# Two feed-forward units woven into the last attention steps, and a new order of the work that follows

## The chip, the cores and the metric

The kernel runs on one core of one Trainium2 chip. The metric is the device time of one execution in microseconds (us); a smaller number is better. A kernel's time is the median of its runs.

## What is computed

Four batches of eight heads go through attention with rotary positions, and the result goes through a SwiGLU layer (a matrix product with a gate weight and one with a value weight, the SiLU of the first times the second, and a product with an output weight). All inputs and outputs are 32-bit floats.

```python
scores = np.matmul(q_rot, k_rot.transpose(0, 1, 3, 2)) / np.sqrt(D)      # 4 x 8 x 576 x 576, D = 64
attn = np.exp(scores - np.max(scores, axis=-1, keepdims=True))
attn = attn / (np.sum(attn, axis=-1, keepdims=True) + 1e-09)
x = np.matmul(attn, v)                      # then transposed and reshaped to 2304 tokens x 512
g = x @ w_gate                              # 512 x 1536
val = x @ w_val                             # 512 x 1536
out = (g * (1 / (1 + np.exp(-g))) * val) @ w_out                         # 1536 x 512
```

## The kernel before, in words

Each 32-bit operand of a product is split into a high and a low part (names that end in `h` and `l`), and a product is the sum of three: high by high, high by low, low by high. ScalarE (ACT) writes the high part by a cast, and VectorE (DVE) or GpSimd (POOL) writes the low part by a subtraction.

**Attention** works on 16 pairs of heads with nine blocks each. A block has scores on TensorE (PE), the negated maximum on DVE (L375), the exponential on ACT (L393), transposes on PE (L436) with their split on ACT and DVE (L437, L438), and the products with the values on PE (`pv_some`, L476, ten matmuls to a group). `pv_evac` copies a finished group to `Y` and stores it to the DRAM tensor `yd`. The row sums become reciprocals `rt`, and `rstore` transposes them, copies them and stores them to the DRAM tensor `rd`.

**The plain stage** (`plain`) computes twelve units: two blocks `f` of 128 of the 1536 columns, by six blocks of 384 tokens, which `UNITS` lists as (f, s, t). A unit is two chains of twelve matmuls (`mm`, L772), one with the gate weight `w0`, one with the value weight `w1`. Then `ev` takes both out of PSUM on ACT: a SiLU (L779), a copy (L780) and one or two stores (L787, L790). PSUM holds three units, so a unit's matmuls wait for the `ev` of the unit three places before it. In the text, ev(u) is the evacuation of unit u. In the listing below, unit 0 is `ps` of `attn_swiglu`.

What stands between the units prepares the next stage:
- `wfirst(1, i)` splits the weights of f = 1. Its DVE part is L733 to L739, its ACT part L720, its POOL part L721 and L722. The raw weights lie in the buffer `raw0`, which `ev` of some units uses afterwards as `sv`.
- `forms` (POOL, L700) makes sums of token blocks in the tiles `T0l0` and `T0l1`, for which `T1` then casts and subtracts (L694). `T0l0` takes over room in which attention's `ET2l` lay.
- `yload` and `rload` fetch attention's results and reciprocals (SyncE's queue, SP). `xlate(t)` scales and splits the token block t = 1 or 2 of the second half (`x1`, `x2` in `plain`; L665 to L680) in small alternating steps of ACT and DVE.
- `Stream` prepares raw weights one block at a time, through two buffers: `load` starts a DMA (L758), `sign` is an ACT operation at the head of a block (L734), and `take` adds the six DVE operations (L735 to L740). `take` signs the next block in the midst of this one unless its second argument is false, and ends with a `load` into the buffer that has come free.
- `sums` (POOL) and `split` (ACT, POOL) make the weights of the first Strassen unit; `forms2` makes `T2`.

**The Strassen stage** (`strassen`, L812) forms the other ten blocks' products from seven products per step. One product is a chain of six matmuls, each chain has one of six PSUM buffers, and DVE's additions (L796) and ACT's copies (L815) free them. **The last stage** (`finish`) multiplies by the output weights.

The order of the work from the end of attention on is written out by hand in `attn_swiglu`, `plain` and `strassen`: each engine takes its instructions in the order in which these functions name them, and an instruction that waits holds up all behind it on its engine. The DMA queues are in order too.

Of the kernel before, what the change touches and what calls it, by code (L numbers as in the profile page):

```python
# [10 lines left out]
FP32 = mybir.dt.float32  # L11
# [112 lines left out]
class Attn:  # L124
# [362 lines left out]
    def store(self, p, half, Y):  # L487
        d = (self.nc.scalar if (p, half) == (B * H // 2 - 1, 1) else self.nc.sync).dma_start
        b, c = divmod(p, 4)
        s, bb = divmod(b, 2)  # L490
        m = s * SG + bb * 512 + 256 * half
        t = s * SG + 1024 + bb * 64
        yd = self.yd[:, 2 * c:2 * c + 2].rearrange("h a d q -> (a d) h q")
        if half == 0:
            d(out=yd[:, :, m:m + 256], in_=Y)
            return
        self.done.add(p)
        Y = Y.rearrange("p h q -> p (h q)")
# [20 lines left out]
class Moe:  # L519
# [113 lines left out]
    def xload(self, s, c, t):  # L633
        o = s * SG + t * BK
        X = self.ld_p.tile([128, 2, BK], FP32, name="Xab")
        for h in range(2):
            self.nc.sync.dma_start(out=X[64 * h:64 * h + 64],
                                   in_=self.yd[h, 2 * c:2 * c + 2, :, o:o + BK].rearrange("a d q -> d a q"))
        return X[:, 0], X[:, 1]

    def xprep(self, s, c, t, ld, eng):
# [4 lines left out]
        self.hicopy(eng, hi, Xa)  # L646
        eng.tensor_tensor(out=lo, in0=Xa, in1=r32(hi), op=ALU.subtract)

    def yload(self, t, c0, c1):
        o = SG + t * BK  # L650
        for h in range(2):
            src = self.yd[h, :, :, o:o + BK].rearrange("(c a) d q -> a d c q", a=2)
            for a, Y in enumerate((self.Ya, self.Yb)):
                self.nc.sync.dma_start(out=Y[64 * h:64 * h + 64, t - 1, c0:c1], in_=src[a, :, c0:c1])

    def xlate(self, t):
        nc = self.nc
# [115 lines left out]
                n += 1  # L773
        return ps

    def ev(self, f, s, t, ps, sv):
        nc = self.nc
        sv = sv.rearrange("p (t i q) -> p t i q", i=2, q=128)
# [183 lines left out]
def attn_swiglu(ctx: ExitStack, tc: tile.TileContext, qk, vr, wg, wv, wo, tab, out):  # L962
    nc = tc.nc
    dr = ctx.enter_context(tc.tile_pool(name="dr", bufs=1, space=bass.MemoryType.DRAM))
    yd = dr.tile([2, 2 * NCH, D, NT], FP32, name="yd")
    rd = dr.tile([B, 36, 128], FP32, name="rd")
    hd = (dr.tile([NFF, 128, FT, 2, 128], FP32, name="hf"), dr.tile([18 - FT, 128, NFF, 2, 128], FP32, name="ht"))
    NP = B * H // 2
# [120 lines left out]
    scx.close()  # L1089
    cctx, xctx = ExitStack(), ExitStack()  # L1090
    moe.open_chain(cctx, 4)
    at.trans(NB - 1)
    at.pv_some(10)
    at.pv_evac()
    at.tails(NP - 1, 1)
    ps = [moe.mm(0, 0, 0, 0)]
    at.pv_some(10)
    at.pv_evac()
    for op in cv1[1]:
        op()  # L1100
# [12 lines left out]
    pl.close()
    moe.open_mid(mctx)
# [11 lines left out]
def run(ops, n=99):  # L1126
    while ops and n:
        ops.pop(0)()
        n -= 1
# [34 lines left out]
        return out  # L1164


def plain(moe, ps):
# [16 lines left out]
    for f in (0, 1, 2, 3, 7, 8, 9, 10, 11):  # L1184
        job("o", f)
    S = Stream(moe, jobs)
    ps, sv = {0: ps}, {}

    def mm(u):
        f, a, t = UNITS[u]  # L1190
        ps[u] = [moe.mm(f, a, t, i) for i in range(2)]

    def ev(u):
        if u % 4 == 0:
            raw = moe.again("raw0", [128, 2, 2 * BK], FP32, "sv")
            sv[u], sv[u + 1] = raw[:, 0], raw[:, 1]
        elif u % 4 > 1:
            sv[u] = moe.ld_p.tile([128, 2, BK], FP32, name="Xab").rearrange("p a q -> p (a q)")
        moe.ev(*UNITS[u], ps.pop(u), sv.pop(u))
# [46 lines left out]
    run(x2)
    ev(7)
    mm(9)
    run(moe.forms2(ve))
# [115 lines left out]
```

## Time and profile before

| quantity | value |
|---|---|
| time, median of 3 runs | 732.16 us (732.03 to 732.17) |
| the profiled execution's own time | 734.16 us |
| its span | 732.4 us |
| PE busy | 703.4 us, 96% of the span |
| DVE busy | 550.8 us, 75% |
| POOL busy | 465.5 us, 64% |
| ACT busy | 405.9 us, 55% |
| PE's share of the chain that ended last | 73% |

The span is the time from the first to the last recorded instruction, and the execution's own time lies 1.8 us above it. The profiled execution took 2.0 us longer than the median run. Busy shares are averages over stages. The granted clock is TensorE's: 1.00 stands for 2.4 GHz and 0.50 for 1.2 GHz, and a value between says how long it was at either.

### The profile page before, as it was taken

To read this page: it belongs to the slowest core of one execution; us is meant where nothing else is said; L and a number is where in the kernel's file an instruction comes from. 1 tells how busy PE (TensorE), PEld (TensorE's weight loads), DVE (VectorE), ACT (ScalarE), POOL (GpSimd) and SP (SyncE) were. 2 spreads that over 40 slices of the span, in tenths; PEclk is the share of its full clock that TensorE was granted. 3 is DMA by queue.
4 is the path that set the end of the run, shared out by engine and by line. 5 is a ranking of instruction groups with operands and counts; after the bars stand their busy time and mean duration, and the time that the engine had idled before them with its cause. 6 is when DMAs were issued, how large, how long until landed. Compare 5 with 4: busy or idle time off the path is not lost.

```text
span 732.4 us, 12724 instructions
## 1 busy us (share of the span) xinstructions
PE 703.4 (96%) x4356; PEld 662.1 (90%) x4356; DVE 550.8 (75%) x898; ACT 405.9 (55%) x884; POOL 465.5 (64%) x462
## 2 busy tenths in 40 slices
PE   6699999999999998988999999999999999999997
PEld 6589999999999998888999999999999977888887
DVE  5799888888888889647987877878766895465451
ACT  2588988888888887336652433324334333333331
POOL 4696989999899957766867675557674857300000
PEclk9999999999999999999999999999999999999999
DMA  4888788779887885783446464665647965787671
GB/s 146 235 204 219 185 191 248 201 200 251 215 207 207 224 208 192 194 225 125 137 145 178 153 188 145 191 183 152 180 123 215 310 250 187 287 278 237 210 216 30
DMA packets 111585, 144.12 MB, mean 197 GB/s; under 512 B 17808, under 2 KB 86432, under 8 KB 111520
## 3 DMA queue, kind: packets, MB, share of 16 engines
q1 hardware_dynamic: 106816, 137.51, 65.5%
q10 hardware_dynamic: 4704, 5.79, 2.4%
q8 instruction: 35, 0.57, 0.3%
q14 instruction: 30, 0.25, 0.1%
HBM read 76.61 MB, written 42.54 MB: 163 GB/s over the span
## 4 chain that ended last, share of the span: by engine, by line
PE 73%; DVE 10%; DMA 6%; ACT 5%; SPq 2%; issue 1%; POOL 1%; ACTq 0%; DVEq 0%; POOLq 0%
PE ch L812 30%; PE ch L929 13%; PE pv L476 9%; PE sc L360 8%; PE tr L436 6%; PE ch L880 3%; DMA HF<-hf 2%; ACT E L393 2%; DVE nmt L375 1%; PE tr L299 1%; DMA X<-in_qk_dram 1%; ACT N L318 1%; DMA hf<-sv 1%; DMA QZ<-N 1%; DVE HF L870 1%
## 5 line engine op out<-in xcount | busy, mean ns | idle before, releaser
L375 DVE TENSOR_REDUCE nmt<-sc 128x1 f32<-128x576 f32 x144 | 108.0, 752 | 21.1 <-PE sc L360 19.9
L393 ACT ACTIVATE E<-sc,nmt 128x576 f32<-128x576 f32 x128 | 97.4, 761 | 11.9 <-DVE nmt L375 10.2
L796 POOL TENSOR_TENSOR u<-u,z 128x384 f32<-128x384 f32 x30 | 30.5, 1016 | 76.6 <-DVE sg L796 76.6
L436 PE MATMUL tr<-ident,E 128*128 128x128 f32 x512 | 77.0, 273 | 0.6 <-DVE N L322 0.6
L815 ACT COPY c<-ch 128x384 f32<-128x384 f32 x30 | 14.4, 481 | 93.2 <-issue 47.1
L360 PE MATMUL sc<-QK 128*128 128x288 f32 x248 | 61.6, 330 | 3.0 <-DMA QK<-N 1.4
L436 PEld LDWEIGHTS tr<-ident,E 128*128 128x128 f32 x512 | 61.3, 141 | 2.8 <-PE tr L299 1.3
L224 POOL TENSOR_TENSOR t<-X,tabs 128x256 f32<-128x256 f32 (+1 forms) x90 | 51.8, 597 | 16.6 <-DMA X<-in_qk_dram 7.2
L694 DVE TENSOR_TENSOR hl<-hg,hh 128x384 fp32r<-128x384 f32 x44 | 25.8, 587 | 38.6 <-ACT hh L694 38.6
L360 PE MATMUL sc<-N,QZ 128*128 128x288 f32 x248 | 53.6, 298 | 1.1 <-DMA QZ<-N 1.1
L929 PE MATMUL ch<-Oh,hh 128*128 128x512 f32 (+1 forms) x144 | 54.0, 375 | 0.0
L437 ACT CAST ET2h<-tr 128x512 fp32r<-128x512 f32 x80 | 47.1, 589 | 12.4 <-PE tr L436 12.4
L929 PE MATMUL ch<-Oh,hl 128*128 128x512 f32 (+1 forms) x144 | 53.9, 374 | 0.0
L929 PE MATMUL ch<-Ol,hh 128*128 128x512 f32 (+1 forms) x144 | 53.8, 374 | 0.0
L438 DVE TENSOR_TENSOR ET2l<-tr,ET2h 128x512 fp32r<-128x512 f32 x80 | 53.1, 683 | 0.6 <-ACT ET2h L437 0.6
L228 POOL TENSOR_TENSOR rot<-rot,t 128x512 f32<-128x512 f32 (+1 forms) x45 | 45.8, 1017 | 3.5
L796 DVE TENSOR_TENSOR sg<-ch,u 128x384 f32<-128x384 f32 x60 | 33.4, 557 | 18.9 <-PE ch L812 15.7
L438 DVE TENSOR_TENSOR ET1l<-tr,ET1h 128x512 fp32r<-128x512 f32 x64 | 42.8, 685 | 6.4 <-ACT ET1h L437 6.2
L437 ACT CAST ET1h<-tr 128x512 fp32r<-128x512 f32 x64 | 36.4, 598 | 17.7 <-PE tr L436 14.5
L227 POOL TENSOR_TENSOR rot<-X,tabs 128x512 f32<-128x512 f32 (+1 forms) x45 | 45.5, 1010 | 0.0
L360 PEld LDWEIGHTS sc<-QK 128*128 128x128 f32 x248 | 38.5, 192 | 6.6 <-ACT E L393 4.6
L694 ACT CAST hh<-hg 128x384 fp32r<-128x384 f32 x44 | 22.6, 514 | 38.5 <-DVE hg L916 38.5
(409 smaller groups left out, 2429.5 us busy)
## 6 DMA issues: line engine op xcount, KB each, us to landing
QK<-N SPq DMA_DIRECT2D x62, 288.0 KB, 4.8
hg<-ht SPq DMA_DIRECT2D x22, 768.0 KB, 6.2
HF<-hf SPq DMA_DIRECT2D x12, 896.0 KB, 5.1
X<-in_qk_dram SPq DMA_DIRECT2D x15, 576.0 KB, 6.7
yd<-Y SPq DMA_DIRECT2D x31, 256.0 KB, 3.8
ht<-sg SPq DMA_DIRECT2D x20, 384.0 KB, 2.9
hf<-sg SPq DMA_DIRECT2D x20, 384.0 KB, 3.6
ht<-sg SPq DMA_DIRECT2D x20, 320.0 KB, 2.8
```

Source lines behind the costliest of these rows:

```text
L224: ins = e.tensor_tensor(out=sel(t2, u), in0=sel(x, w), in1=tb(Sn, u), op=ALU.mult)
L360: nc.tensor.matmul(ps[:, g, 0:288], l, rr[:, o + g * 288:o + (g + 1) * 288], start=(x == 0), stop=(x == len(terms) - 1))
L375: nc.vector.tensor_reduce(out=nmcol, in_=ps[:, :, 0:288], axis=AX.XY, op=ALU.max, negate=True)
L393: nc.scalar.activation(out=E.rearrange("p (a b) -> p a b", a=2), in_=ps[:, :, 0:288], func=ACTF.Exp, bias=nmcol, scale=1.0, accum_out=self ...
L436: nc.tensor.transpose(ps[:, c], E[:, o + c * 128:o + (c + 1) * 128], self.ident)
L437: nc.scalar.copy(dst[0], src)
L438: nc.vector.tensor_tensor(out=dst[1], in0=src, in1=r32(dst[0]), op=ALU.subtract)
L476: nc.tensor.matmul(st["ps"][:, 0:w], VS[:, sl, :], t, start=(x == 0), stop=(x == last))
L694: return [lambda: self.nc.scalar.copy(h, f), lambda: le.tensor_tensor(out=l, in0=f, in1=r32(h), op=ALU.subtract)]
L796: add = lambda e, out, in0, in1: e.tensor_tensor(out=out, in0=in0, in1=in1, op=ALU.add)
L812: nc.tensor.matmul(acc, l[:, w, c * 128:(c + 1) * 128], r, start=(n == 0), stop=(n == 5))
L929: self.nc.tensor.matmul(ps, l[:, f], r[:, z], start=(n == 0), stop=(n == 3 * NFF - 1))
```

## The change

It touches the last steps of attention and the plain stage.
- The first unit's gate chain moves ahead of attention's last transposes, and its value chain ahead of the last two groups of `pv`. The second unit, (0, 0, 1), which was the first one in `plain`, is now woven around the last group: its gate chain ahead of it and its value chain behind it. `ev` of unit 0 and `rstore` stand between the two groups of `pv`.
- `yd` becomes two DRAM tensors, of six and of two of its eight rows per half. `rload` for t = 1 moves ahead of the later `yload` calls.
- The rest of the preparation of w1 of f = 1 (`cv1[1]`, now `first`) moves from the end of attention into `plain`, behind the `forms` and the first `sign`.
- `ev` decides itself which buffer it writes: units 2, 3, 8 and 9 share `raw0`, the others take buffers of `ld_p`.
- Of the stream's weight blocks, one stood in the middle of the stage; it now stands at the end, where two follow each other. `x1` and `x2` move ahead of `T1`, of the splits of the Strassen weights and of `forms` for the first half.

```diff
-    yd = dr.tile([2, 2 * NCH, D, NT], FP32, name="yd")
+    yd = [dr.tile([2, n, D, NT], FP32, name=f"yd{n}") for n in (6, 2)]
...
+    ps = [moe.mm(0, 0, 0, 0)]
     at.trans(NB - 1)
     at.pv_some(10)
     at.pv_evac()
     at.tails(NP - 1, 1)
-    ps = [moe.mm(0, 0, 0, 0)]
+    ps.append(moe.mm(0, 0, 0, 1))
+    at.pv_some(10)
+    moe.ev(0, ps)
+    at.pv_evac()
+    at.rstore(B - 1)
+    ps = [moe.mm(0, 0, 1, 0)]
     at.pv_some(10)
     at.pv_evac()
-    for op in cv1[1]:
-        op()
-    ps.append(moe.mm(0, 0, 0, 1))
-    at.pv_some(10)
-    at.pv_evac()
-    at.rstore(B - 1)
+    ps.append(moe.mm(0, 0, 1, 1))
...
+        if u in (2, 8):
+            raw = self.again("raw0", [128, 2, 2 * BK], FP32, "sv")
+            self.sv = [raw[:, 1], raw[:, 0]]
+        if u in (2, 3, 8, 9):
+            sv = self.sv.pop()
+        else:
+            sv = self.ld_p.tile([128, 2, BK], FP32, name="Xab").rearrange("p a q -> p (a q)")
...
     for c in range(2):
         run(moe.forms(1, c, moe.Z[c], po))
     x1, x2 = moe.xlate(1), moe.xlate(2)
-    mm(1)
+    mm(2)
     S.sign()
-    ev(0)
-    mm(2)
+    run(first)
     run(S.take(1))
     ev(1)
     mm(3)
...
     S.load()
     S.load()
-    for t in (1, 2):
-        moe.yload(t, 0, 3)
-    for t in (1, 2):
-        moe.yload(t, 3, 4)
-        moe.rload(1, t, moe.R12 if t == 2 else None)
+    moe.yload(1, 0)
+    moe.rload(1, 1)
+    moe.yload(2, 0)
+    moe.yload(1, 1)
+    moe.rload(1, 2, moe.R12)
+    moe.yload(2, 1)
...
     mm(4)
-    T1(0)
-    run(x1, 3)
     ev(3)
     mm(5)
-    run(x1)
+    run(x1, 5)
     ev(4)
     mm(6)
-    T1(1)
-    S.sign()
-    run(S.take(1, False))
-    w = [J[0].split(x, po) for x in range(2)]
-    run(w[0])
+    run(x1)
     ev(5)
     mm(7)
-    run(w[1])
+    T1(0)
     run(x2, 3)
     ev(6)
     mm(8)
+    w = [J[0].split(x, po) for x in range(2)]
+    run(w[0])
+    run(x2, 2)
+    ev(7)
+    mm(9)
+    run(w[1])
+    run(x2)
+    T1(1)
...
-    S.sign()
     ev(9)
     mm(11)
+    S.sign()
     run(S.take(1))
     ev(10)
+    run(S.take(1))
     run(J[1].sums(po))
     ev(11)
```

**POOL at the end of attention.** `w1h` and `w1l` are the halves of w1 of f = 1, `T0l` the tiles of the two `forms` (the number tells the two tiles apart), `WF` that of `sums`. Before:

```order
L721 TENSOR_TENSOR raw<-raw,w1h_4089 128x512
L722 TENSOR_TENSOR w1l_4090<-raw 128x512
L700 TENSOR_TENSOR T0l_4436<-xa1h,xa1l 128x2x384
L700 TENSOR_TENSOR T0l_4436<-xm1h,xm1l 128x384
L700 TENSOR_TENSOR T0l_4436<-xb1h,xb1l 128x384
L700 TENSOR_TENSOR T0l_4436<-T0l_4436 128x768
L700 TENSOR_TENSOR T0l_4436<-T0l_4436 128x384 x2
```

And of the change:

```order
L701 TENSOR_TENSOR T0l_4458<-T0l_4458 128x384 x2
L701 TENSOR_TENSOR T0l_4459<-xa1h,xa1l 128x2x384
L701 TENSOR_TENSOR T0l_4459<-xm1h,xm1l 128x384
L701 TENSOR_TENSOR T0l_4459<-xb1h,xb1l 128x384
L701 TENSOR_TENSOR T0l_4459<-T0l_4459 128x768
L701 TENSOR_TENSOR T0l_4459<-T0l_4459 128x384 x2
L722 TENSOR_TENSOR raw<-raw,w1h_4090 128x512
L723 TENSOR_TENSOR w1l_4091<-raw 128x512
L958 TENSOR_TENSOR WF_4456<-WF_4456 128x256
```

The two operations that finish w1 of f = 1 stood ahead of both `forms`; they moved behind the last of their twelve operations.

**ACT at the end of the plain stage**, from ev(9) to ev(11). `aux<-raw` is a block's `sign`, `ACTIVATE sv<-ch` or `Xab<-ch` with its `COPY` is an `ev`, and `c<-ch` is the Strassen stage's first copy. Before:

```order
L734 ACTIVATE aux<-raw 128x512
L779 ACTIVATE sv<-ch 128x3x128
L780 COPY sv<-ch 128x3x128
L790 DMA ht<-sv 128x3x256
L734 ACTIVATE aux<-raw 128x512
L779 ACTIVATE Xab<-ch 128x3x128
L780 COPY Xab<-ch 128x3x128
L790 DMA ht<-Xab 128x3x256
L779 ACTIVATE Xab<-ch 128x3x128
L780 COPY Xab<-ch 128x3x128
L790 DMA ht<-Xab 128x3x256
L815 COPY c_4981<-ch 128x384
```

And of the change:

```order
L788 ACTIVATE sv<-ch 128x3x128
L789 COPY sv<-ch 128x3x128
L799 DMA ht<-sv 128x3x256
L735 ACTIVATE aux<-raw 128x512 x2
L788 ACTIVATE Xab<-ch 128x3x128
L789 COPY Xab<-ch 128x3x128
L799 DMA ht<-Xab 128x3x256
L735 ACTIVATE aux<-raw 128x512
L788 ACTIVATE Xab<-ch 128x3x128
L789 COPY Xab<-ch 128x3x128
L799 DMA ht<-Xab 128x3x256
L824 COPY c_4983<-ch 128x384
```

Before, one `sign` stood ahead of ev(9) and one ahead of ev(10). Now none stands ahead of ev(9), two stand ahead of ev(10), and a third stands between ev(10) and ev(11).

**DVE at the start of the Strassen stage.** `T2l` is the last result of `forms2`, `WF` that of a weight block, and `u<-ch` the first addition of the Strassen stage. Before:

```order
L709 TENSOR_TENSOR T0h<-T0h 128x768
L694 TENSOR_TENSOR T2l<-T0h,T2h 128x2x768 x2
L735 TENSOR_SCALAR aux<-aux 128x512
L736 TENSOR_SCALAR aux<-aux 128x512
L737 SCALAR_TENSOR_TENSOR raw<-raw,aux 128x512
L738 TENSOR_SCALAR aux<-raw 128x512
L739 SCALAR_TENSOR_TENSOR aux<-raw,aux 128x512
L740 TENSOR_TENSOR WF_4435<-raw,aux 128x512
L796 TENSOR_TENSOR u<-ch,c_4981 128x384
```

And of the change, from `forms2` to the end of the first weight block; six more operations of the second block follow, and then the same `u<-ch`:

```order
L695 TENSOR_TENSOR T1l<-T0l_4459,T1h 128x4x384
L710 TENSOR_TENSOR T0h<-T0h 128x768
L695 TENSOR_TENSOR T2l<-T0h,T2h 128x2x768 x2
L736 TENSOR_SCALAR aux<-aux 128x512
L737 TENSOR_SCALAR aux<-aux 128x512
L738 SCALAR_TENSOR_TENSOR raw<-raw,aux 128x512
L739 TENSOR_SCALAR aux<-raw 128x512
L740 SCALAR_TENSOR_TENSOR aux<-raw,aux 128x512
L741 TENSOR_TENSOR WF_4457<-raw,aux 128x512
```

Two blocks of six operations now stand between `T2l` and `u` where one stood, and the second half of `T1l` has come ahead of `forms2`.

## Rows read from the trace of the kernel before

**Rows 1.** Windows: us; busy of PE, PEld, DVE, ACT, POOL (x instructions); clock; DMA.

```profile
360.00:380.00 20.00, 20.00 (x117) 20.00 (x116) 18.62 (x31) 10.82 (x15) 16.39 (x12) 1.00 0.45 138
...
291.00:295.00 4.00, 4.00 (x18) 4.00 (x16) 3.41 (x6) 0.97 (x2) 3.23 (x3) 0.57 0.22 66
...
325.00:329.00 4.00, 3.74 (x12) 3.74 (x13) 2.37 (x5) 2.70 (x8) 0.00 (x0) 0.57 1.13 281
...
341.00:345.00 4.00, 3.17 (x12) 3.18 (x13) 3.33 (x7) 2.42 (x6) 3.92 (x4) 0.69 0.58 199
```

**Rows 2.** Timeline of PE: start, us, instruction, idle time before it and its releaser.

```profile
290.58 0.66 PE L436 MATMUL tr<-ident,Et 128*128 128x128 f32 x4 [1.86 <-ACT Et L393]
...
298.61 0.31 PE L476 MATMUL pv<-ET2h,VS 128*128 128x320 f32 x1
...
306.06 0.44 PE L772 MATMUL ch<-xa1h,w0h 128*128 128x384 f32 x1 [1.56 <-ACT sv L779]
...
310.33 0.34 PE L772 MATMUL ch<-xa0h,w0h 128*128 128x384 f32 x1
...
325.26 0.53 PE L772 MATMUL ch<-xm1h,w0h 128*128 128x384 f32 x1 [2.29 <-ACT Xab L779]
...
341.82 0.44 PE L772 MATMUL ch<-xa2h,w0h 128*128 128x384 f32 x1 [2.06 <-ACT Xab L779]
...
357.67 0.35 PE L812 MATMUL ch<-xa1h,W0h 128*128 128x384 f32 x1
```

**Rows 3.** Timeline of POOL, the same columns.

```profile
300.71 1.54 POOL L721 TENSOR_TENSOR raw<-raw,w1h 128x512 f32<-128x512 f32 x1 [3.98 <-ACT w1h L720]
...
303.60 1.82 POOL L700 TENSOR_TENSOR T0l<-xa1h,xa1l 128x768 f32<-128x768 f32 x1
...
311.42 1.86 POOL L700 TENSOR_TENSOR T0l<-xa1h,xa1l 128x768 f32<-128x768 f32 x1
...
339.99 1.81 POOL L700 TENSOR_TENSOR R<-xa0h,xa0l 128x768 f32<-128x768 f32 x1
...
358.22 1.01 POOL L700 TENSOR_TENSOR Z<-Z 128x384 f32<-128x384 f32 x1
```

**Rows 4.** Timeline of DVE, the same columns.

```profile
293.36 0.63 DVE L438 TENSOR_TENSOR ET2l<-tr,ET2h 128x512 fp32r<-128x512 f32 x1
...
314.25 2.60 DVE L694 TENSOR_TENSOR T1l<-T0l,T1h 128x1536 fp32r<-128x1536 f32 x1 [1.37 <-ACT T1h L694]
...
323.35 0.57 DVE L667 TENSOR_TENSOR aux<-aux,R 128x384 f32<-128x384 f32 x1 [6.03 <-DMA R<-rd]
...
330.75 0.56 DVE L675 TENSOR_TENSOR xa2l<-aux,xa2h 128x384 fp32r<-128x384 f32 x1 [0.47 <-ACT T0h L674]
...
333.40 1.76 DVE L694 TENSOR_TENSOR T1l<-T0l,T1h 128x1536 fp32r<-128x1536 f32 x1 [2.09 <-ACT T1h L694]
...
339.32 0.56 DVE L666 TENSOR_TENSOR aux<-aux,T2h 128x384 f32<-128x384 f32 x1
...
349.73 1.72 DVE L709 TENSOR_TENSOR T0h<-T0h 128x768 f32<-128x768 f32 x1
...
357.19 0.69 DVE L735 TENSOR_SCALAR aux<-aux 128x512 f32<-128x512 f32 x1
...
361.43 0.55 DVE L796 TENSOR_TENSOR u<-ch,c 128x384 f32<-128x384 f32 x1
```

**Rows 5.** Timeline of ACT and its queue, the same columns.

```profile
331.89 1.48 ACT L694 CAST T1h<-T0l 128x1536 fp32r<-128x1536 f32 x1 [0.40 <-ACT sv L780]
...
333.84 1.04 ACT L694 CAST W0h<-WF 128x1024 fp32r<-128x1024 f32 x1
...
356.01 0.64 ACT L734 ACTIVATE aux<-raw 128x512 f32<-128x512 f32 x1 [0.44 <-ACT sv L780]
```

**Rows 6.** DMA: line L758's times to landing; the waits of SP's queue, 285 to 372.

```profile
DMA to landing us min/median/max: 3.2/3.7/7.0
...
SPq L654 <- DMA hf<-sv: 6.8, 1, 6.8
```

More of the change, by code (lines that the diff above doesn't have):

```diff
@@ L492, in store @@
         t = s * SG + 1024 + bb * 64
-        yd = self.yd[:, 2 * c:2 * c + 2].rearrange("h a d q -> (a d) h q")
+        yd = self.yd[c // 3][:, 2 * (c % 3):2 * (c % 3) + 2].rearrange("h a d q -> (a d) h q")
         if half == 0:
@@ L637, in xload @@
             self.nc.sync.dma_start(out=X[64 * h:64 * h + 64],
-                                   in_=self.yd[h, 2 * c:2 * c + 2, :, o:o + BK].rearrange("a d q -> d a q"))
+                                   in_=self.yd[c // 3][h, 2 * (c % 3):2 * (c % 3) + 2, :, o:o + BK].rearrange("a d q -> d a q"))
         return X[:, 0], X[:, 1]
@@ L647, in xprep, with yload @@
         eng.tensor_tensor(out=lo, in0=Xa, in1=r32(hi), op=ALU.subtract)
-    def yload(self, t, c0, c1):
+    def yload(self, t, i):
         o = SG + t * BK
+        z = slice(3 * i, 3 + i)
         for h in range(2):
-            src = self.yd[h, :, :, o:o + BK].rearrange("(c a) d q -> a d c q", a=2)
+            src = self.yd[i][h, :, :, o:o + BK].rearrange("(c a) d q -> a d c q", a=2)
             for a, Y in enumerate((self.Ya, self.Yb)):
-                self.nc.sync.dma_start(out=Y[64 * h:64 * h + 64, t - 1, c0:c1], in_=src[a, :, c0:c1])
+                self.nc.sync.dma_start(out=Y[64 * h:64 * h + 64, t - 1, z], in_=src[a])
     def xlate(self, t):
@@ L774, in mm, with ev @@
         return ps
-    def ev(self, f, s, t, ps, sv):
+    def ev(self, u, ps):
         nc = self.nc
+        f, s, t = UNITS[u]
+        if u in (2, 8):
[5 more added lines that the diff above has]
+            sv = self.ld_p.tile([128, 2, BK], FP32, name="Xab").rearrange("p a q -> p (a q)")
         sv = sv.rearrange("p (t i q) -> p t i q", i=2, q=128)
@@ L1110, in attn_swiglu @@
     moe.open_aux(xctx, 2)
-    J, S, Z = plain(moe, ps)
+    J, S, Z = plain(moe, ps, cv1[1])
     mctx.close()
@@ L1164, in take, with plain @@
         return out
-def plain(moe, ps):
+def plain(moe, ps, first):
     nc = moe.nc
@@ L1186, in plain @@
     S = Stream(moe, jobs)
-    ps, sv = {0: ps}, {}
+    ps = {1: ps}
     def mm(u):
-        f, a, t = UNITS[u]
-        ps[u] = [moe.mm(f, a, t, i) for i in range(2)]
+        ps[u] = [moe.mm(*UNITS[u], i) for i in range(2)]
     def ev(u):
[L1194 to L1199, printed above, removed]
+        moe.ev(u, ps.pop(u))
     def T1(c):
@@ L1245, in plain @@
         run(moe.forms(0, c, Z[c], po))
[L1246 to L1249, printed above, removed]
+    T2 = moe.forms2(ve)
+    run(T2, 2)
     ev(8)
     mm(10)
-    S.sign()
+    run(T2)
     ev(9)
     mm(11)
+    S.sign()
     run(S.take(1))
     ev(10)
+    run(S.take(1))
     run(J[1].sums(po))
```

## The prediction

> **What bounds the kernel now.** I read the windows of all engines first, then PE's timeline around the end of attention, then the timelines of the engines that it waits for. In the Strassen stage PE is full: 117 matmuls in 20.0 us, so a chain of six takes 1.03 us, at a granted clock of 1.00 [rows 1]. Whatever moves the start of that stage therefore moves the end of the kernel by as much. The plain stage ahead of it isn't full. A unit of two chains needs 4.16 us (306.06 to 310.33, less 0.11 for its slow first matmul), but PE stands still for 1.86 us ahead of the last transposes, and for 1.56, 2.29 and 2.06 us ahead of units that find no free PSUM buffer because ACT is late with an evacuation [rows 2]. That is 7.8 us. The granted clock tells the rest: after three of these waits it is 0.57 to 0.69 over four microseconds, between its levels of 1.2 and 2.4 GHz, and twelve matmuls take 3.74 us in place of 2.08 [rows 1]. Such a stretch costs 1.66 us. What made ACT late is on DVE: the first scaling of a late token block waits 6.0 us for the reciprocals `R` [rows 4].
>
> So there is something to win, nearly 13 us with the three slow stretches, and the change aims at the right waits. The question is what waits instead. The orders printed above answer it, and each later step is taken from them.
>
> **The sum, step by step.** Times are on the profile's own axis.
>
> 1. *End of attention.* The chain that now stands ahead of the last transposes covers the 1.86 us wait, and with it goes the slow stretch, 1.66 us. One more chain, 2.08 us, comes ahead of the last group of `pv`, and the transposes of the reciprocals, 0.1 us. The first of the two groups now comes so early that it waits for `ET2l`, which DVE ends at 293.99 [rows 4]: 0.6 us. So the last group starts at 298.61 [rows 2] - 1.86 - 1.66 + 2.08 + 0.1 + 0.6 = 297.9 in place of 298.6. The stores of `rd` and the loads of `R` come several microseconds earlier and are nobody's last wait any more. Splitting `yd` by itself I cost at nothing: its bytes and its DMA count are the same, and where a load may start earlier nobody waits for it.
>
> 2. *POOL.* The first `forms` writes into room that `ET2l` held, so it waits for eight matmuls of that last group, 1.2 us: 299.1. One `forms` took 7.82 us (303.60 to 311.42) [rows 3], two take 15.6, to 314.7. Only then come the two operations that finish w1 of f = 1. They took 2.89 us (300.71 to 303.60) [rows 3], so `w1l` is there at 317.6. Before, it was there at 303.6.
>
> 3. *PE waits for it.* From 297.9 PE does the ten `pv` matmuls (1.5), the second unit's value chain (2.1), unit 2 (4.2), a chain and two matmuls of unit 3 (2.4): it stands at 308.1, until 317.6. What step 1 wins therefore counts only through POOL's start. Ten matmuls of the broken chain follow at the lower clock, 3.2 us, and eight units, 33.3 us. The Strassen stage could start at 354.2, against 357.67 [rows 2]: 3.5 us earlier.
>
> 4. *ACT and DVE behind it.* ev(2) writes to `raw0`, where w1's raw weights lie, so ACT waits for `w1l` too, and then, in ev(3), for the chain that ends at 320.9. The first addition of `x1` starts at about 322.5. `x1` took 8.0 us (323.35 to 331.31): 330.5. ev(5) and the cast of `T1h` (331.89 to 333.40 before [rows 4, 5]) come first again, 2.9 us, then `T1l`, 1.76 us: 335.1. `x2` took 10.4 us (339.32 to 349.73) and now has two casts of `W0h` in ACT's stream, some 0.95 us each from start to start of 1.04 us: 347.4. The second `T1l` comes next; beside a working POOL it took 2.60 us, else 1.76 [rows 4]. I take 2.60, since POOL does the other `forms` then: 350.0. `forms2` with both `T2l` took 7.46 us (349.73 to 357.19): 357.5. The six operations of the first weight block took 4.24 (357.19 to 361.43 [rows 4]): 361.7. Before, one such block had been done in the middle of the stage.
>
> 5. *The load behind it.* The third `sign` needs raw weights whose DMA can be issued only when this block has freed its buffer. Such a load takes 3.7 us (3.2 to 7.0) [rows 6]: 365.4. The sign itself takes 0.64 [rows 5], and ev(11) stands behind it on ACT with 0.48: its first buffer is free at 366.5. PE needs that buffer for the fifth chain of the Strassen stage, at 354.2 + 4.1 = 358.3. It stands still for 8.2 us and then runs a slow stretch, 1.66 us more.
>
> Before, the fifth chain began at 357.67 + 4.1 = 361.8. Now its equal is 366.5 + 1.66 = 368.2. The sum is +6.4 us. DVE's second weight block, ahead of `u`, ends at about 366 and frees the eighth chain's buffer by 367; since PE comes there after 370, it adds nothing. The profiled execution took 734.16 us and would take 740.6; the median of the runs lies 2.0 us below it, so I predict 732.16 + 6.4 = 738.6 us.
>
> *Unknown prices.* ACT's stores and SP's loads share eight completion counters, and one DMA waits until the eighth before it has landed: SP once stood 6.8 us for a store of ACT's [rows 6]. With the new order three of ACT's stores stand behind loads of `yd` and `rd`. ACT had no such wait before, so I take 0 and keep 6.8 as the other end. The casts of `W0h` may be hidden (-1.9), DVE may meet less of POOL (0.84 at `T1l`; `T2l` at `T1l`'s 1.76 each, with half of `forms2`, some 3 us), the load may take 3.2 (-0.5) or 7.0 (+3.3).
>
> *Two rules beside the rows.* `forms` on POOL met DVE's weight operations from 304 to 311 and took 7.82 us; the pair from 339.99 to 359.23 [rows 3], beside `forms2` and `T2l`, took 19.2, against 15.6. The Trainium skill, "SBUF — State Buffer", section "SBUF: two separate sides", says that GpSimd and VectorE share a pair of ports as an exclusive lock that is held for the whole instruction. The longer pair agrees with it, the shorter one shows no trace of it. By the lock the `forms` of step 2 would take up to 19.2 us; that is the second rival.
> For step 5, the row's median is 3.7 us. The Trainium skill, "DMA: Bandwidth & Descriptors", section "Anatomy of one DMA — SWDGE (gpsimd) path", fits 2.0 us plus bytes over 436e3 for another issuing path. For 512 KB I estimate 3.2 us from it, the row's minimum, and the sum would be +5.9.
>
> **The rivals.**
> - *The load isn't waited for, so the kernel is faster.* If ACT and DVE run through `x1`, `x2` and `forms2` with hardly a gap, the first weight block ends early enough for the load to land before PE's fifth chain, and only step 3 counts: -3.5 us, 728.7. It decides from there: step 4's chain has to end by 353.5 in place of 361.7. For it: the work alone, without gaps, is about 31 us of the 39 that I count. Against it: `x1` and `x2` took 8.0 and 10.4 us before, with the same ping-pong between the two engines, and nothing in the change shortens it. 8 in 100.
> - *`forms` takes 19.2 us.* POOL's operations of step 2 meet DVE's weight operations. Everything behind is 3.6 us later: +10.0, 742.2. Against it is the first pair of before, beside the same kind of work. 8 in 100.
> - *About the same.* Half of step 4's gaps go and the collisions with them, some 6 us: +0.4, 732.6. 11 in 100.
> - *The change does what its order is for*, since POOL is quick and w1 is never waited for: the four waits and slow stretches go, and about 9 of 13 us come through: 723. The printed order of POOL speaks against it. 3 in 100.
>
> **How the numbers follow.** 0.2% is 1.5 us, about what a measurement of this kernel can tell from no change. The forecast has 70 in 100, and with the second rival the slower cases have 78. Same has 11, faster 8 + 3 = 11. The range leaves out the faster cases and the far end of slow loads: 733.5, where the third rival begins to turn into the forecast with a few of the low ends, to 743.0, which takes in the second rival. About 18 in 100 lie outside.
>
> **What would show it.** POOL's first `forms` starts near 299 and `w1l` ends near 317.6; PE has one wait of nearly 10 us for POOL's `w1l`, near 308; ACT's first `sv` starts with it. PE waits a second time, near 358, for an evacuation into `Xab`, some 8 us, and ACT's longest wait there is for the DMA of raw gate weights. The granted clock falls after both. The wait of DVE for `R` is gone. The prediction is wrong if `w1l` is ready before 312, or if ACT's third sign doesn't wait for its load.

## The result: 1.2% slower, by two waits in a row

| quantity | before | after |
|---|---|---|
| time, median of 4 runs | 732.15 us (732.03 to 732.17) | 741.00 us (740.53 to 741.51) |
| ratio of the times, 95% interval | 1 | 1.0121 (1.0104 to 1.0139) |
| the profiled execution's own time | 734.16 us | 741.51 us |
| its span | 732.4 us | 739.7 us |
| PE busy | 703.4 us, 96% | 699.4 us, 95% |
| DVE busy | 550.8 us | 553.1 us |
| POOL and ACT busy | 465.5 and 405.9 us | 465.6 and 405.8 us |

The change costs 8.85 us. No engine has more work to do: DVE is busy 2.3 us longer, POOL and ACT within 0.1 us of before, and the time is idle time of PE. The last `ET2l` of attention ends at 292.01 in the profile of after and ended at 293.99 in that of before [rows 4]; so 2.0 us are to be taken off a time on before's axis before it is set beside one of after. On that common axis the profiled spans differ by 739.7 - 730.4 = 9.3 us.

### The profile after

The waits, 285 to 375 us: who waited for whom, us in total, times, longest.

```profile
ACT sv L788 <- POOL w1l L723: 13.7, 1, 13.7
...
PE ch L773 <- POOL w1l L723: 10.4, 1, 10.4
ACT aux L735 <- DMA raw<-in_moe_w_gate_dram: 9.2, 1, 9.2
...
PE ch L821 <- ACT Xab L788: 8.2, 1, 8.2
```

PE waits twice, 10.4 and 8.2 us. Before, it had five waits: the four of 1.56 to 2.29 us [rows 2], and one of 1.09 us at 353.40 that the prediction leaves out. Each of the two waits of after goes with a longer one of ACT, for POOL's `w1l` and for the load of raw gate weights. DVE no longer waits for `R`, as it did for 6.0 us [rows 4].

The timeline of PE over the same stretch: only these instructions were waited for by PE or start a stage.

```profile
292.07 0.41 PE L476 MATMUL pv<-ET2l,VS 128*128 128x320 f32 x1 [0.26 <-DVE ET2l L438]
...
316.43 0.69 PE L773 MATMUL ch<-xa0h,w1l 128*128 128x384 f32 x1 [10.45 <-POOL w1l L723]
...
353.29 0.35 PE L821 MATMUL ch<-xa1h,W0h 128*128 128x384 f32 x1
...
365.83 0.69 PE L821 MATMUL ch<-T1h,W0h 128*128 128x384 f32 x1 [8.18 <-ACT Xab L788]
```

The wait of 1.86 us ahead of the last transposes [rows 2] is gone, as the change intends. The Strassen stage starts at 353.29, against 357.67 - 2.0 = 355.67 before: 2.4 us earlier in spite of the wait of 10.45 us. Everything is lost again, and more, at its fifth chain.

The granted clock in both places, by windows (columns as in [rows 1]):

```profile
312.00:316.00 4.00, 0.00 (x0) 0.00 (x0) 0.63 (x1) 0.00 (x0) 3.84 (x4) 0.50 1.10 232
316.00:320.00 4.00, 3.57 (x11) 3.57 (x12) 0.00 (x0) 0.86 (x2) 3.17 (x5) 0.50 1.04 205
...
364.00:368.00 4.00, 2.17 (x7) 2.17 (x8) 1.72 (x3) 2.83 (x5) 3.84 (x6) 0.50 0.42 107
368.00:372.00 4.00, 4.00 (x16) 4.00 (x15) 3.42 (x4) 2.19 (x3) 1.36 (x3) 0.57 0.36 127
```

After both waits the granted clock is 0.50, and matmuls run at 1.2 GHz: 11 of them, from 316.43 to 320.11, and 17, from 365.83 to 371.44. At 0.173 us for one at the full clock they would have taken 1.91 and 2.95 us, so the stretches cost 1.8 and 2.7 us.

Now the engines that PE waits for. POOL:

```profile
297.10 1.85 POOL L701 TENSOR_TENSOR T0l<-xa1h,xa1l 128x768 f32<-128x768 f32 x1 [2.33 <-PE pv L476]
...
306.00 1.82 POOL L701 TENSOR_TENSOR T0l<-xa1h,xa1l 128x768 f32<-128x768 f32 x1
...
315.09 1.29 POOL L723 TENSOR_TENSOR w1l<-raw 128x512 fp32r<-128x512 f32 x1
...
361.33 3.97 POOL L701 TENSOR_TENSOR Z<-Z 128x768 f32<-128x768 f32 x3
```

The two operations of w1 stand behind both `forms`, the first of them at 313.73, and `w1l` ends at 316.38; before it ended at 303.60 [rows 3]. The last row is to be kept in mind: the other `forms`, `R` and `Z`, end at 365.28.

ACT, its first wait and its last:

```profile
316.41 0.49 ACT L788 ACTIVATE sv<-ch 128x384 f32<-128x384 f32 x1 [13.74 <-POOL w1l L723]
...
364.74 0.64 ACT L735 ACTIVATE aux<-raw 128x512 f32<-128x512 f32 x1 [9.16 <-DMA raw<-in_moe_w_gate_dram]
365.31 0.48 ACT L788 ACTIVATE Xab<-ch 128x384 f32<-128x384 f32 x1
...
366.96 1.48 ACT L695 CAST T0h<-Z 128x1536 fp32r<-128x1536 f32 x1
```

DVE from `T2l` on, and SyncE's queue:

```profile
350.81 5.89 DVE L695 TENSOR_TENSOR T2l<-T0h,T2h 128x1536 fp32r<-128x1536 f32 x2
356.62 0.69 DVE L736 TENSOR_SCALAR aux<-aux 128x512 f32<-128x512 f32 x1
...
360.87 0.69 DVE L736 TENSOR_SCALAR aux<-aux 128x512 f32<-128x512 f32 x1
...
367.16 0.56 DVE L805 TENSOR_TENSOR u<-ch,c 128x384 f32<-128x384 f32 x1 [1.96 <-ACT c L824]
```

```profile
360.98 4.58 SPq L759 DMA_DIRECT2D raw<-in_moe_w_gate_dram  x2
```

The first weight block ends where the second begins, at 360.87. At 360.98 its free buffer's load is issued, 3.8 us later the third `sign` starts on ACT (364.74), behind it ev(11) (365.31), and PE's fifth chain (365.83). That is the chain that the prediction forecast. Such a load is 512 KB for 128 x 512 weights: the weights reach the kernel as 64-bit floats, not as the 32-bit ones named at the start.

### The profile page after: what moved, and what is told of

Its sections match the earlier page's. It is cut to its first block, busy times and chain, and to the rows that moved or that the text cites. A ratio compares the mean times of both kernels' runs of the same rounds, so it can differ in the third digit from the quotient of the medians.

```text
span 739.7 us, 12726 instructions
## 1 busy us (share of the span) xinstructions
PE 699.4 (95%) x4356; PEld 659.5 (89%) x4356; DVE 553.1 (75%) x898; ACT 405.8 (55%) x884; POOL 465.6 (63%) x462
## 4 chain that ended last, share of the span: by engine, by line
PE 73%; DMA 9%; DVE 8%; ACT 4%; POOL 3%; issue 1%; SPq 1%; ACTq 0%; DVEq 0%; POOLq 0%
PE ch L821 29%; PE ch L938 12%; PE pv L476 10%; PE sc L360 9%; PE tr L436 7%; PE ch L889 3%; DMA X<-in_qk_dram 2%; DMA HF<-hf 2%; PE tr L299 2%; DMA raw<-in_moe_w_gate_dram 2%; DMA raw<-in_moe_w_val_dram 1%; ACT E L393 1%; ACT N L318 1%; POOL t L224 1%; DVE HF L879 1%
```

## The experiments

Theory: the loss is made of two waits, one behind the other. POOL's order makes the first, the load of the third `sign` the second, and each is undone by moving one thing. Rivals: the first wait is slack that is waited away later anyway; ACT's or DVE's own work, not the load, is what is late; the split of `yd` or the weaving itself costs. No run puts `x1` and `x2` back behind `T1`, so what that part of the new order is worth stays open. The ratio is that to the kernel before, with its 95% interval; the kernel before took 731.7 to 732.6 us beside them. In the profiles attention ends at different times, as it does between before and after. Where two of them are compared below, the difference at the last `ET2l` is taken off.

| run | time, us | ratio |
|---|---|---|
| e1: w1 ahead of `forms` | 733.07 | 1.0010 (1.0000 to 1.0021) |
| e2: third `sign` later | 737.79 | 1.0086 (1.0069 to 1.0102) |
| e3: one block in the middle | 741.72 | 1.0131 (1.0107 to 1.0155) |
| e4: one `yd` | 741.09 | 1.0129 (1.0113 to 1.0144) |
| e5: e3 and `T0` later | 746.42 | 1.0184 (1.0158 to 1.0211) |
| e6: e1, e3 and `T0` later | 742.70 | 1.0152 (1.0125 to 1.0178) |
| e7: e1, e3 and early `R`, `Z` | 729.68 | 0.9969 (0.9955 to 0.9984) |
| e8: e7 and `T0` later | 737.27 | 1.0068 (1.0049 to 1.0088) |
| e9: e7 and another order of loads | 726.74 | 0.9929 (0.9907 to 0.9952) |
| e10: e7, middle block later | 727.16 | 0.9927 (0.9896 to 0.9959) |
| e11: e9 without the weaving | 732.78 | 0.9998 (0.9979 to 1.0016) |
| e12: e10, middle block later still | 725.89 | 0.9922 (0.9897 to 0.9946) |

### e1: w1 ahead of the forms

```diff
+    run(first)
     for c in range(2):
         run(moe.forms(1, c, moe.Z[c], po))
...
     S.sign()
-    run(first)
     run(S.take(1))
```

> The changed kernel, with the two GpSimd operations that finish w1 of f = 1 ahead of both forms again. Theory (two waits, the first made by GpSimd's order): w1l ends near 302 in place of 316.4, PE's wait of 10.4 us in unit 3 and the slow stretch behind it (about 1.7 us) go, the chain on ScalarE and VectorE moves forward with it, and the second wait, at the fifth chain of the Strassen stage, stays at 8 us, give or take 2. Time 741.0 - 12 = 729, between 727 and 732. Rival (the chain on VectorE is held by something else, such as the reciprocals R or GpSimd's forms, so that the time is only waited away later): the second wait grows to 14 us or more and the time stays between 736 and 741.

Measured: 733.07 us, 7.9 less than the change and 1.1 above the expected range. Timeline of PE, the first and the last of its waits from 322 on:

```profile
335.93 0.44 PE L773 MATMUL ch<-xb2h,w0h 128*128 128x384 f32 x1 [0.58 <-ACT xb2h L673]
...
358.54 0.69 PE L821 MATMUL ch<-T1h,W0h 128*128 128x384 f32 x1 [8.22 <-ACT Xab L788]
```

The wait for `w1l` is gone with its slow stretch (10.45 + 1.8), the chain on ACT and DVE moved forward with it, and the second wait kept its size, 8.22 us against 8.18. That is the theory, and not its rival, by which the second wait would have grown to 14 us. Three new waits (0.58, 0.80 and 0.61 us) stand where PE now asks for the parts of `x2` as they are made. So the edit is worth 12.2 - 2.0 = 10.2 us on paper. The two profiled executions differ by 8.0, and attention, which the edit doesn't touch, ends 1.6 us later in this one (the last `ET2l` at 293.64 against 292.01): 9.6. Shown: POOL's order alone makes a loss of about 8 us by the medians.

### e2: the third sign later

```diff
     ev(10)
-    run(S.take(1))
+    run(S.take(1, False))
...
+    at(0, 0, 2, S.sign)
```

> The changed kernel, with the third sign behind ev(11) and two copies of the Strassen stage. Theory (the sign that waits for its load is what holds ev(11)): no wait of PE at the fifth chain; the first u on VectorE, behind two weight blocks that end near 365, becomes the bound, so PE stands some 4 to 5 us at the eighth chain; the time is 736 to 738.5. Rival (ev(11) is late by itself, because its matmuls or ScalarE's other work end late): ScalarE's wait for the load goes, the fifth chain still waits about 8 us, time 740 to 742.

Measured: 737.79 us, as the theory had it. Its waits, 285 to 376:

```profile
ACT T0h L695 <- POOL Z L701: 7.6, 1, 7.6
...
PE ch L821 <- DVE u L805: 4.3, 1, 4.3
```

The wait for ev(11) is gone, so the `sign` behind its load held it. PE runs on to the eighth chain and waits there for `u`, 4.3 us: only 3.2 us were won. `u` starts as soon as DVE's second weight block ends, at 365.8, so that block is the bound now. ACT shows a wait that was hidden: 7.6 us for POOL's `Z`.

### e3: one weight block in the middle again

```diff
+    S.sign()
+    run(S.take(1, False))
     T1(0)
     run(x2, 3)
...
     ev(10)
-    run(S.take(1))
     run(J[1].sums(po))
```

> The changed kernel, with one of the two last weight blocks in the middle again, behind x1, as in the kernel before. Theory: the load of the third sign is issued some 20 us before it is needed, the wait of 8.2 us and the slow stretch behind it (2.5 us) go, u starts near 361 in place of 367 and costs PE at most 1 us; the wait of 10.4 us in unit 3 stays. Time 741.0 - 10 = 731, between 730 and 733. Rival (the middle has no room: the block makes x2 and the evacuations behind it late): new waits of PE in units 6 to 11, time 735 to 741.

Measured: 741.72 us, no gain at all. The theory's 731 is a clear miss. The rival's time came mostly for another reason than its own: the new waits in units 6 to 11 that it names come to 1.9 us. Two waits of this run, and PE's timeline from 361 on:

```profile
ACT T0h L695 <- POOL Z L701: 7.6, 1, 7.6
...
PE ch L821 <- ACT z L824: 4.5, 1, 4.5
```

```profile
362.62 0.44 PE L821 MATMUL ch<-xa2h,W0h 128*128 128x384 f32 x1 [0.72 <-DVE u L805]
368.46 0.69 PE L821 MATMUL ch<-T2h,W0h 128*128 128x384 f32 x1 [4.52 <-ACT z L824]
```

The load isn't waited for any more and the fifth chain runs. `u` starts at 362.02 in place of 367.16; attention ends 2.2 us earlier in this profile, so 2.9 us of that are the edit's. But behind ACT's first copy `c` stands the cast `T0h<-Z`; it waits until POOL has made `Z`, at 366.5, and the copy `z` that frees the next buffer stands behind the cast. So **three** chains of work end within 0.6 us of each other in the changed kernel: the load that the `sign` waits for (364.74), DVE's second block (365.2), POOL's `Z` (365.28). Taking away one uncovers the next. The middle block even makes the third one later, by 3.4 us with the 2.2 taken off, since ACT waits for the block before it casts `W0h`, and POOL's `R` and `Z` stand behind `W0l`.

### e4: yd as one tensor

```diff
-    yd = [dr.tile([2, n, D, NT], FP32, name=f"yd{n}") for n in (6, 2)]
+    yd = dr.tile([2, 2 * NCH, D, NT], FP32, name="yd")
...
```

> The changed kernel with yd as one DRAM tensor again. Theory (the split is worth nothing, since what follows the loads waits for w1l until 316): between 740 and 742, no new wait. Rival (the split brings the loads of yd and rd forward, and this is worth something): SyncE's loads start 3 us or more later, VectorE waits for R or Ya, and the time is 743 or more.

Measured: 741.09 us against 741.00. The lines left out address the one tensor. The split neither costs nor gives anything in this order of the work.

### e5, e6, e8: the casts T0 later

All three have e3's edit; e6 and e8 have e1's too, and e8 that of e7 below. In common:

```diff
-    at(0, 0, 1, T0(1))
-    at(0, 0, 4, T0(0))
+    at(0, 1, 2, T0(1))
+    at(0, 1, 5, T0(0))
```

> The changed kernel with one weight block in the middle again (as in the run before it) and, beside that, the two casts T0h and the subtractions T0l of the Strassen stage eleven and eight chains later, so that ScalarE's cast T0h, which waits for GpSimd's forms Z, no longer stands ahead of the copy z. Theory (three chains of work end within a microsecond of each other near 365: the sign behind its load, GpSimd's Z, and VectorE's second block; taking away one uncovers the next, and with two away the third is short): PE has no wait over 1.5 us in the first chains of the Strassen stage; time 730 to 733. Rival (VectorE, not ScalarE's order, is what is late): PE waits 4 us or more for u or sg there, time 736 to 741.

> The same as the run with the block in the middle and the later T0, and w1 of f = 1 finished ahead of both forms. Theory (the two waits are independent of each other, both go): no wait of PE for w1l; 8 to 9 us less than the run with w1 first alone (733.1), 2 to 4 us of it given back, since VectorE's x2 and last block now hold units 8 to 11 and the eighth chain: 722 to 728. Rival (VectorE's chain of x1, x2, forms2 and two blocks is the bound as soon as w1l is early, so that the block in the middle costs what it gives): 730 to 734.

> Both at once: w1 first, the block in the middle, GpSimd's forms R and Z ahead of W0l, and T0 later. Theory (either of the last two is enough by itself): within 1.5 us of the better of the two runs that have one of them, 721 to 727. Rival (the two hold different waits): at least 2 us below both.

Measured: 746.42, 742.70 and 737.27 us. All three are misses: e5 is 4.7 us slower than e3 by this edit alone, and e8 is 7.6 slower than e7. Timelines of ACT and of PE in e5:

```profile
372.51 1.04 ACT L695 CAST W1h<-WF 128x1024 fp32r<-128x1024 f32 x1 [4.12 <-POOL WF L961]
...
375.56 1.45 ACT L695 CAST T0h<-Z 128x1536 fp32r<-128x1536 f32 x1
```

```profile
379.00 0.44 PE L821 MATMUL ch<-T0h,W0h 128*128 128x384 f32 x1 [1.40 <-ACT T0h L695]
...
383.70 0.69 PE L821 MATMUL ch<-T0l,W0h 128*128 128x384 f32 x1 [4.26 <-DVE T0l L695]
```

The cast moved out of one queue's way into another's: it now stands behind the cast `W1h`, which waits for POOL's sums, and those stand behind `Z` as well. It starts at 375.56, 6.8 us later than in e3 with the difference of the axes (2.2) taken off, and the third unit of the Strassen stage waits for `T0h` and `T0l`. What was late in e3 is POOL; ACT's order can't mend that.

In e8 `Z` is early, and nothing on ACT waits for POOL there. PE waits for `T0l` just as long (4.26 us), so the later place costs by itself. ACT in e8, and a wait of PE's there:

```profile
361.62 2.00 ACT L695 CAST W1h<-WF 128x1024 fp32r<-128x1024 f32 x2
...
365.37 1.47 ACT L695 CAST T0h<-Z 128x1536 fp32r<-128x1536 f32 x1
```

```profile
PE ch L821 <- DVE T0l L695: 4.3, 1, 4.3
```

e6 and e8 have besides a wait of PE's ahead of unit 8, 9.5 and 8.7 us. e7 shows where that one comes from.

### e7: the forms R and Z earlier

This one mends POOL. With e1's and e3's edits:

```diff
     T1(0)
+    Z = [moe.r_p.tile([128, 4, BK], FP32, name="R"), moe.again("T0l0", [128, 4, BK], FP32, "Z")]
+    for c in range(2):
+        run(moe.forms(0, c, Z[c], po))
     run(x2, 3)
...
-    Z = [moe.r_p.tile([128, 4, BK], FP32, name="R"), moe.again("T0l0", [128, 4, BK], FP32, "Z")]
-    for c in range(2):
-        run(moe.forms(0, c, Z[c], po))
```

> w1 first and the block in the middle, T0 where it was, and instead GpSimd's two forms of the first half (R and Z) ahead of W0l, right behind the first T1. Theory (GpSimd's Z ends some 18 us earlier, near 340, and T0h no longer waits): ScalarE's wait for Z is gone, 722 to 728, the same as with T0 later within 2 us. Rival (W0l is late in its place, since it now stands behind 15.6 us of forms): PE waits 2 us or more for W0l at the first chains of the Strassen stage, 728 to 733.

Measured: 729.68 us, faster than the kernel before, and 1.7 above the range. The time lies in the rival's range, but its wait for `W0l` isn't there. No wait for `Z` is left, and the Strassen stage has no wait of PE in its first chains. The edit does a second thing that this run can't tell apart: it takes the `forms` out of DVE's way, and `T2l` takes 3.41 us in place of 5.89. The rest is one wait ahead of it. PE, SyncE's queue and a wait of ACT's:

```profile
335.08 0.69 PE L773 MATMUL ch<-xa2h,w0h 128*128 128x384 f32 x1 [7.99 <-ACT Xab L788]
```

```profile
321.05 0.45 SPq L655 DMA_DIRECT2D T2h<-yd  x1
321.60 1.08 SPq L759 DMA_DIRECT2D raw<-in_moe_w_val_dram  x2
```

```profile
326.00 0.63 ACT L735 ACTIVATE aux<-raw 128x512 f32<-128x512 f32 x1 [6.41 <-DMA raw<-in_moe_w_val_dram]
```

With w1 ready early ACT has done all ahead of the middle block's `sign` at 319.6, but the load for it is issued at 321.60 only: it stands behind the loads of `yd` and `rd` in SyncE's queue, of which the first row is the last one. DVE had freed the buffer at 303.3.

### e9 and e10: the load earlier, or the sign later

e9 puts the two weight loads ahead of the loads for `x2`; e10 leaves SyncE's queue as it is and moves the block behind ev(6):

```diff
     moe.yload(1, 0)
     moe.rload(1, 1)
-    moe.yload(2, 0)
     moe.yload(1, 1)
-    moe.rload(1, 2, moe.R12)
-    moe.yload(2, 1)
...
     run(S.take(1, False))
+    moe.yload(2, 0)
+    moe.rload(1, 2, moe.R12)
+    moe.yload(2, 1)
```

```diff
-    S.sign()
-    run(S.take(1, False))
     T1(0)
...
     ev(6)
     mm(8)
+    S.sign()
+    run(S.take(1, False))
```

> The run with w1 first, the block in the middle and the early forms R and Z, and beside it SyncE's order changed: the last loads of yd for the block x1 come ahead of those for x2, and the loads for x2 (and its reciprocals) stand behind the two weight loads of the stream. Theory (there the sign in the middle waits 6.4 us because its weight load stands in SyncE's queue behind 18 loads of yd and rd, and lands near 326 only): the load lands near 313 to 315, ScalarE's wait of 6.4 us and PE's of 8.0 with its slow stretch of 3 us go: 729.7 - 11 = 718.5, between 716 and 723. Rival (the loads for x2 are late in place of it): VectorE or ScalarE waits for T0h or T2l ahead of x2, PE waits 3 us or more in units 8 to 11, 724 to 730.

> The same run as a start (w1 first, early forms), SyncE's order untouched, and the middle block's sign behind ev(6) and three steps of x2. Theory (the sign only has to come later than 326, so that nothing on ScalarE stands behind a wait for it): the wait of 8.0 us goes, at the price of 1 to 3 us in units 9 to 11: 719 to 724. Rival (ScalarE then waits for loads of x2 just as long, since they land after 321 as well): 726 to 731.

Measured: 726.74 and 727.16 us. Both gain 2.5 to 3 us on e7, where 6 to 14 were expected, and both lie in their rivals' ranges. In e9 the weight loads are issued at 310.60 and the sign still starts late. ACT, its own queue's rows among them, and PE:

```profile
318.87 0.50 ACT L789 COPY Xab<-ch 128x384 f32<-128x384 f32 x1
325.71 0.33 ACTq L796 DMA_DIRECT2D hf<-Xab  x1
...
326.77 0.63 ACT L735 ACTIVATE aux<-raw 128x512 f32<-128x512 f32 x1 [7.40 <-DMA T2l<-rd]
```

```profile
335.86 0.69 PE L773 MATMUL ch<-xa2h,w0h 128*128 128x384 f32 x1 [6.85 <-ACT Xab L788]
```

The store of ev(5), which needs nothing but the copy at 318.87, is issued 6.3 us after that copy's end. It waits for a load of `rd` that SyncE issued: in the trace's records the two have the same completion counter, one of eight that the DMAs of both queues use here, and a DMA waits until the one before it on its counter has landed. The prediction bounded this price by 0 and 6.8 us [rows 6]. In the changed kernel it is 1.9 us (the copy ends at 317.27, the store is issued at 319.19) and hidden; here it takes the place of the wait for the load. In e10 no such wait of ACT's is longer than 1.9 us, but the block stands inside `x2`: a copy of `x2` on ACT waits 3.4 us for it, the evacuation behind that copy is late, and PE waits 3.16 us for it and 1.33 for `xb2h`, with a slow stretch of 2.2.

### e11: the weaving taken out

e9 with the end of attention as in the kernel before:

```diff
-    ps = [moe.mm(0, 0, 0, 0)]
     at.trans(NB - 1)
...
     at.tails(NP - 1, 1)
-    ps.append(moe.mm(0, 0, 0, 1))
+    ps = [moe.mm(0, 0, 0, 0)]
     at.pv_some(10)
-    moe.ev(0, ps)
     at.pv_evac()
-    at.rstore(B - 1)
-    ps = [moe.mm(0, 0, 1, 0)]
+    for op in cv1[1]:
+        op()
+    ps.append(moe.mm(0, 0, 0, 1))
     at.pv_some(10)
     at.pv_evac()
-    ps.append(moe.mm(0, 0, 1, 1))
+    at.rstore(B - 1)
...
+    mm(1)
     S.sign()
+    ev(0)
+    mm(2)
```

> The first of these two kernels with the end of attention as in the kernel before: both chains of unit 0 behind the last transposes, ev(0) and the second unit behind attention. Theory (the weaving itself is worth the wait of 1.86 us ahead of the last transposes, its slow stretch of 1.66, and the earlier ev(0)): 3 to 6 us slower than the kernel with the weaving. Rival (the weaving is worth nothing, because the stage is held by loads and ScalarE and not by when PE begins it): within 1.5 us of it.

Measured: 732.78 us, 6.0 more than e9, at the upper end of what was expected. The wait of 1.9 us ahead of the transposes is back, and one of 2.1 us ahead of unit 2 for an evacuation. Shown: with the other repairs of e9 in place, the weaving is worth some 6 us; in the change more than that is used up.

### e12: the block behind x2

e10 with the block later still, and four small loads of `yd` exchanged:

```diff
     run(w[1])
     run(x2)
+    S.sign()
+    run(S.take(1, False))
     T1(1)
...
     moe.rload(1, 1)
+    moe.yload(1, 1)
     moe.yload(2, 0)
-    moe.yload(1, 1)
```

> w1 first, the forms R and Z early, the middle block behind all of x2 and ahead of the second T1, and the last loads of yd for x1 issued ahead of the first for x2 (four DMAs change places with four, so that every other DMA keeps its place). Theory (what is left of the loss in the run with the later block is VectorE's block inside x2, 4.3 us, and the load of yd that the last copy of x1 waits for, 2.9 us): PE's waits in units 10 and 11, 5.6 us with their slow stretch of about 3, shrink to 2 us; the weight load has landed by 331 and nobody waits for it; the first u is the bound and costs 0 to 2 us: 727.2 - 6 = 721, between 718 and 724. Rival (VectorE has the same work in all of these orders and its end, the first u near 353, sets the time): the wait only moves to the eighth chain of the Strassen stage, 725 to 729.

Measured: 725.89 us, the fastest of all, 0.8% below the kernel before, but within the intervals of e9 and e10. The rival's range holds it: waits were exchanged, not removed. Two of PE's waits in it:

```profile
337.46 0.69 PE L773 MATMUL ch<-xb2l,w0h 128*128 128x384 f32 x1 [0.60 <-DVE xb2l L676]
...
348.27 0.44 PE L821 MATMUL ch<-xa1h,W0h 128*128 128x384 f32 x1 [2.45 <-ACT sv L788]
```

Ahead of the Strassen stage PE waits 1.7 us (0.32, 0.81 and 0.60) in place of e10's 5.5, and a new wait stands at the start of that stage: ev(9) stands on ACT behind a cast `T2h` that waits 5.2 us for DVE. The first `u` starts at 353.97, in e10 at 353.67. With POOL and the loads mended, DVE's and ACT's work from `x1` to `u` takes 44 us in both orders, and its end stays. Whether a shorter order of that work exists was not tried.

## Why the prediction was right, and where it was off

The forecast was 738.6 us, the result 741.0: the sign and the mechanism are right, the size is 2.4 us short of 8.85. By its number alone the result is nearer to the second rival, 742.2; it is the trace that decides for the forecast. By its own steps, on after's axis (its times less 2.0):

1. *End of attention.* The last group of `pv` was to start at 295.9; it starts at 295.69, and the wait for `ET2l` is 0.26 us in place of 0.6. Right.
2. *POOL.* The first `forms` starts at 297.10, as said. `w1l` ends at 316.38 in place of 315.6. This term was mis-sized: the first `forms` took 8.90 us (297.10 to 306.00), not the 7.82 taken over from before. It met DVE's w1 operations, as the last section shows; the second one took 7.73.
3. *PE waits.* From 305.98 to 316.43, where 306.1 to 315.6 was said. The slow stretch has 11 matmuls in place of ten. The Strassen stage starts at 353.29, where 352.2 was said.
4. *ACT and DVE.* `x1` starts at 321.92 (said: 320.5), the first weight block ends at 360.87 (said: 359.7). The delay of POOL and some 0.6 us more pass straight through; the durations between are right within half a microsecond each.
5. *The load.* The sign starts at 364.74 (said: 363.4), 3.8 us after the issue, where 3.7 was taken. The fifth chain starts at 365.83 (said: 364.5). The stretch behind it was mis-sized: 17 slow matmuls cost 2.7 us, not the 1.66 of ten.

So 6.4 + 1.3 (0.8 of it from step 2, carried through) + 1.0 (the stretch) = 8.7 of 8.85. Of the 9.3 us between the profiles 0.6 are left; they lie in the last stage, behind the path of the five steps.

One reading of the kernel before is wrong without harm to the sum. The prediction puts ACT's late evacuations down to DVE's wait for `R`, but PE's wait at 306.06 comes 11 us before that wait begins (323.35 - 6.03 = 317.3).

The rival by which the load isn't waited for fails by 9 us at its own criterion: step 4's chain was to end by 353.5 (351.5 on this axis) and ended at 360.87. The rival by the port lock asked for two `forms` of 19.2 us; they took 16.6, where the forecast had 15.6. It was a right rule in a wrong place, as the last section shows.

What the prediction didn't see is that step 5 is not alone. It treated the wait for the load as the bound of the stage, and costed DVE's second block at nothing behind it; both hold for the sum. But undoing step 5 gives 3.2 us in e2, where DVE's second block holds PE next, and nothing in e3, where POOL's `Z` does, which no step mentions and which ends as late as the load. A sum that is nearly right for the change would have been wrong by 10 us for its repair. My expectations for e3, e5, e6 and e8 were: the times lie 9 to 15 us above their ranges.

## What to carry to other kernels

Work that is pulled forward on one engine is only as early as the in-order queues that feed it: here two short POOL operations behind 15.6 us of others, one `sign` ahead of an evacuation, and in e7 a weight load behind 18 small ones. Ahead of a move, list for each queue what the moved work now stands behind. And before repairing a wait, look for what else ends within a few microseconds of it: three chains ended together here, so that each single repair of the second wait gave little or nothing.

## What the runs showed of the hardware

**VectorE and GpSimd hold each other up, but only for some operations.** DVE's part of w1, beside POOL's first `forms` in the changed kernel, and in e1, where POOL stands idle; in both the first and the last of four operations:

```profile
297.28 1.96 DVE L737 TENSOR_SCALAR raw<-raw 128x512 uint32<-128x512 uint32 x1
...
301.87 2.22 DVE L740 SCALAR_TENSOR_TENSOR raw<-raw 128x512 f32<-128x512 uint32 x1
```

```profile
298.77 0.43 DVE L737 TENSOR_SCALAR raw<-raw 128x512 uint32<-128x512 uint32 x1
...
300.42 0.69 DVE L740 SCALAR_TENSOR_TENSOR raw<-raw 128x512 f32<-128x512 uint32 x1
```

The four take 6.70 us (1.96, 1.39, 1.13, 2.22) in place of 2.24, and the first `forms` takes 1.1 us more than before. The operations of the weight blocks, whose `aux` lies in PSUM, take 0.69 to 0.70 us each, beside a busy POOL (356.62 to 365.2 in the changed kernel) as well as beside an idle one (351.15 to 355.49 in e7). The other pair is exact. POOL's last three operations of `R` and DVE's `T2l`, in e1, where they meet, and in e7, where they don't:

```profile
342.86 7.44 POOL L701 TENSOR_TENSOR R<-R 128x768 f32<-128x768 f32 x3
```

```profile
343.52 5.91 DVE L695 TENSOR_TENSOR T2l<-T0h,T2h 128x1536 fp32r<-128x1536 f32 x2
```

```profile
323.60 4.02 POOL L701 TENSOR_TENSOR R<-R 128x768 f32<-128x768 f32 x3
```

```profile
347.69 3.41 DVE L695 TENSOR_TENSOR T2l<-T0h,T2h 128x1536 fp32r<-128x1536 f32 x2
```

Where they meet, POOL takes 3.42 us longer, which is what DVE's two operations need by themselves. The Trainium skill, "SBUF — State Buffer", section "SBUF: two separate sides", says that the shared pair of ports is held for a whole instruction, and that on DVE's side only a two-port mode or two inputs in SBUF ask for it, the latter only against a GpSimd operation that reads SBUF. The traces agree in both halves, with the 3.42 us above and the unchanged 0.69 to 0.70; which mode an operation runs in they don't tell. The prediction used the first half alone, and so looked for the lock at the weight blocks, which have a PSUM operand.

**Neither the length of a wait nor the sum of several tells how long PE runs slowly behind it.** The granted clock was 0.50 in each of these stretches. The wait for `w1l`, 10.44 us here and 10.45 in the changed kernel, had 17 slow matmuls behind it in e2 and 11 in the changed kernel. In e2:

```profile
316.87 0.69 PE L773 MATMUL ch<-xa0h,w1l 128*128 128x384 f32 x1 [10.44 <-POOL w1l L723]
```

Behind the 8.2 us at the fifth chain 17 ran at 1.2 GHz in the changed kernel and 18 in e1 (358.54 to 364.46). The three short waits of e12 (0.32, 0.81 and 0.60 us) had nine behind them (337.46 to 340.51), while the same three places in e1 (0.58, 0.80 and 0.61 us) had none: there the granted clock stayed at 1.00 from 334 to 344. It also stayed at 1.00 behind the single wait of 2.45 us in e12. Where the clock fell, the stretches cost 1.5 to 2.9 us each.
